# A second spectrum buffer, another priority and a last matmul group by column halves, in a one-core FFT convolution with gated MLP

## The chip, the cores and the metric

The kernel runs on one core of one Trainium2 chip. The metric is the device time of one launch in microseconds (us). A core has a matrix engine (TensorE, PE in the profile; PEld is its weight load), a vector engine (VectorE, DVE), a scalar engine (ScalarE, ACT), GpSimd (POOL), and SyncE (SP), which here only issues transfers.

## The reference

Two sequential blocks with pre-normalisation on a sequence of 2048 rows and 640 channels, in bf16:

```python
x = A_u                                           # (1, 2048, 640)
h  = x + conv(layernorm(x))                       # state space kernel K, applied by FFT of length 4096
h2 = h + ((sigmoid(n @ w_gate) * (n @ w_up)) @ w_down)   # n = layernorm(h), inner width 1728
```

The kernel works on four blocks of 512 rows. The convolution of a block is a product of spectra (inputs Z, kernel spectra S) followed by an inverse transform on TensorE; for block 0 that happens in four channel chunks of 160 (numbered 0 to 3), interleaved with the tail of the making of K. The MLP of a block follows when its normalisation is ready.

## The kernel before

A scheduler orders the instructions of each engine by priority and by its own idea of when they become ready. The order in the engine queues is then fixed at build time.

The product spectrum V of one chunk of block 0 has one buffer (tag `t3`, one slot), so chunk c+1 may write V only when the inverse transform of chunk c has read it:

```python
def prod(c, fs):
    if not fs[0]:
        T["y", c] = prp.tile([P, 2, 2, 2, W], BF16, name="V", tag="t3", bufs=1)
    ...
    V(g(t1[:, f]), z, k, ALU.mult)                               # L536
    V(g(t2[:, f]), z, k[:, :, ::-1], ALU.mult)                   # L537
    V(y[:, f, :, 0], t1[:, f, :, 0], t1[:, f, :, 1], ALU.subtract)   # L538
    V(y[:, f, :, 1], t2[:, f, :, 0], t2[:, f, :, 1], ALU.add)        # L539
```

The last chunk is done at a raised priority, and statistics of the chunks that are already finished are put in around it:

```python
    for r in range(4):
        for q in range(NC - 2):                     # chunks 0 and 1
            nc.vector.bn_stats(st2[:, r, q, :], h[:, r, W * q:W * q + W])   # L712
    tc.cur_priority += int(AT["EARLY"])
    piece(1, 0, 0, ...)                             # first piece of block 1's products: L693 to L704
    tc.cur_priority -= int(AT["EARLY"])
    tc.cur_priority -= int(AT["TAIL"])              # 64
    spec(c, 0, 0)
    spec(c, 0, 1)
    prod(c, (0,))                                   # first half of V of chunk 3
    prod(c, (1,))                                   # second half
    tc.cur_priority += int(AT["TAIL"])
    ... # bn_stats of chunk 2 (L723); then the inverse, with bn_stats of chunk 3 straight from PSUM (L727)
```

The last stage of the MLP is the down projection. Its output for a row group of 128 rows has two column halves of 320, in the two banks of one PSUM tile:

```python
po = [[t[:, c] for c in range(2)] for t in (pso_p.tile([P, 2, 512], F32, ...) for _ in range(2))]
def chunks(k, start, stop):
    lr = lp + k
    for ft in range(FT):                            # 13
        for c in range(2):
            nc.tensor.matmul(po[k][c][:, 0:320], lhsT=hm[:, ft, ...], rhs=Wd[:, ft, 320 * c:320 * c + 320], ...)
...
    for k in range(2):
        for c in range(2):
            nc.vector.tensor_tensor(h2[:, c], ..., h2[:, c], ALU.add)
        if b == NB - 1:
            nc.sync.dma_start(oh[b, :, lr:lr + 1, :], hs[b][:, lr:lr + 1, :])
```

## Time and profile before

| | before |
|---|---|
| time, median of the first 3 runs (range) | 356.66 us (356.56 to 356.86) |
| span of the profiled execution | 355.0 us |
| busy: PE, DVE, ACT | 320.4, 283.3, 245.9 us |
| last L341 to the L727 statistics | 125.87 to 144.34: 18.47 us |
| L727 to the end of the last matmul | 144.34 to 351.42: 207.08 us |
| end of the last matmul to the end of the span | 351.42 to 355.0: 3.58 us |

The mark "last L341" is the last instruction of the K tables on VectorE; up to 120 us, shortly ahead of it, nothing that the change edits has run (the first is chunk 1's V, at 120.76).

Lines that come up often: L536 and L537 make the factors of V, the product of spectra, and L538 and L539 V itself; L565 are the matmuls of the inverse transform (ps_y) and L568 is ScalarE's copy of their result; L518 are the matmuls that make the kernel's spectra and L522 ScalarE's copies of these (S, xk); L580 is a small product for the block's edge, which the inverse also needs; L712, L723 and L727 are statistics; L693 to L704 belong to block 1; L909 are the gate (ml_pg) and up (ml_pu) matmuls of the MLP.

The lines that the change moves are these, from the timeline of VectorE of the kernel before. The columns are start, length, engine, line, operation, output and inputs, forms and count; brackets at the end tell how long the engine was idle before and what ended it.

```profile
141.13 0.32 DVE L539 TENSOR_TENSOR V<-t 128x320 bf16<-128x320 bf16 x1
141.47 0.23 DVE L580 TENSOR_TENSOR edge<-edge,uhead 1x160 bf16<-1x160 bf16 x1
141.73 0.49 DVE L702 TENSOR_TENSOR early<-VR 128x640 bf16<-128x640 bf16 x1
142.14 0.32 DVE L723 BATCH_NORM_STATS2 ln_st<-h 128x6 f32<-128x160 bf16 x1
142.38 0.88 DVE L704 TENSOR_TENSOR VR<-early 128x640 bf16<-128x640 bf16 x2
143.17 0.77 DVE L723 BATCH_NORM_STATS2 ln_st<-h 128x6 f32<-128x160 bf16 x3
144.34 1.03 DVE L727 BATCH_NORM_STATS2 ln_st<-ps_y 128x6 f32<-128x160 f32 x4 [0.40 <-PE ps_y L565]
```

V of chunk 3 is whole at about 141.45; the edge product, L702 and the two L704 stand behind it and run while TensorE makes the inverse. L727 starts when TensorE has finished, after 0.40 us of idleness.

### The profile page before, as it was taken

The page shows a single profiled execution, that of the slowest core. Times are in us where ns is not written, and L with a number is a line of the kernel's source. Part 1 is how long each engine was busy: PE and PEld are TensorE (multiplying, and loading weights), DVE is VectorE, ACT ScalarE, POOL GpSimd, SP SyncE. Part 2 cuts the span into 40 slices and gives each one's busy share as a digit, 9 for nine tenths or more (in the row PEclk, how much of TensorE's full clock was granted, in tenths as well). Part 3 has the DMA queues.
Part 4 walks back from the last instruction along what each step waited for, and adds up shares of the span by engine and source line. Part 5 has one row for each costly group of instructions (what it writes and reads, how often), then busy time and mean ns, then how long its engine had stood idle before and what let it go on. Part 6 is the DMA issues. An engine that isn't in the chain of part 4 may idle for free.

```text
span 355.0 us, 6617 instructions
## 1 busy us (share of the span) xinstructions
PE 320.4 (90%) x2584; PEld 204.0 (57%) x2584; DVE 283.3 (80%) x570; ACT 245.9 (69%) x455; POOL 11.4 (3%) x20
## 2 busy tenths in 40 slices
PE   2587989997799999899999899998899999999995
PEld 1464667765487778755456554555554456544463
DVE  3899999999898799879999899999899951211222
ACT  6999999998999764673767845547844678455500
POOL 1020002200000000100000100000100001000000
PEclk9998999999999999999999999999999999999999
DMA  6990000454205339989500053000012000400011
GB/s 172 323 404 4 15 2 2 113 179 157 76 3 160 137 88 352 289 273 280 227 4 0 5 179 113 3 0 0 3 74 76 0 1 11 133 7 1 0 37 38
DMA packets 32391, 35.00 MB, mean 99 GB/s; under 512 B 19676, under 2 KB 27741, under 8 KB 32104
## 3 DMA queue, kind: packets, MB, share of 16 engines
q1 hardware_dynamic: 32360, 34.59, 30.7%
q8 instruction: 20, 0.33, 0.4%
q14 instruction: 11, 0.09, 0.1%
HBM read 24.70 MB, written 9.21 MB: 96 GB/s over the span
## 4 chain that ended last, share of the span: by engine, by line
DVE 28%; PE 18%; issue 14%; ACT 2%; POOL 1%; POOLq 0%; DVEq 0%; ACTq 0%
DVE u L694 5%; PE ml_po L942 5%; DVE u L693 5%; PE ml_pg L909 5%; PE ml_pu L909 4%; DVE u L696 3%; DVE u L697 3%; DVE ml_hm L920 2%; DVE VR L704 2%; PE ps_y L565 1%; DVE Z L673 1%; DVE y L701 1%; DVE y L702 1%; DVE h L805 1%; ACT ln L859 1%
## 5 line engine op out<-in xcount | busy, mean ns | idle before, releaser
L909 PE MATMUL ml_pg<-lnT,Wg 128*128 128x512 bf16 x260 | 64.6, 379 | 0.2 <-ACT ml_sg L917 0.2
L909 PE MATMUL ml_pu<-lnT,Wu 128*128 128x512 bf16 x260 | 64.4, 379 | 0.0
L942 PE MATMUL ml_po<-Wd,ml_hm 128*128 128x320 bf16 x416 | 59.5, 299 | 1.7 <-ACT Wd L963 1.7
L942 PEld LDWEIGHTS <-ml_hm 128*128 128x128 bf16 x416 | 40.1, 98 | 19.6 <-issue 3.7
L917 ACT ACTIVATE ml_sg<-ml_pg 128x512 bf16<-128x512 f32 x52 | 30.9, 597 | 25.5 <-PE ml_pg L909 11.9
L920 DVE TENSOR_TENSOR ml_hm<-ml_ub,ml_sg 128x512 bf16<-128x512 bf16 x52 | 22.0, 423 | 28.0 <-ACT ml_ub L919 28.0
L909 PEld LDWEIGHTS <-Wu 128*128 128x128 bf16 x260 | 25.4, 98 | 30.7 <-issue 0.3
L919 ACT CAST ml_ub<-ml_pu 128x512 bf16<-128x512 f32 x52 | 30.4, 584 | 17.0 <-PE ml_pu L909 16.9
L909 PEld LDWEIGHTS <-Wg 128*128 128x128 bf16 x260 | 25.4, 98 | 28.8 <-issue 0.4
L457 PE MATMUL ps_z<-u,c_G 128*128 128x320 bf16 x192 | 30.3, 307 | 4.5 <-ACT zs L458 2.7
L518 PE MATMUL ps_xk<-kv,c_KM 128*128 128x160 bf16 x320 | 27.0, 232 | 1.8 <-ACT S L522 0.8
L693 DVE TENSOR_TENSOR u<-Z,S 128x1280 bf16<-128x1280 bf16 x34 | 27.8, 820 | 0.0
L694 DVE TENSOR_TENSOR u<-Z,S 128x1280 bf16<-128x1280 bf16 x34 | 27.8, 820 | 0.0
L457 PEld LDWEIGHTS <-c_G 128*128 128x128 bf16 x192 | 18.9, 99 | 13.7 <-issue 6.0
L518 PEld LDWEIGHTS <-c_KM 128*128 128x128 bf16 x320 | 23.5, 98 | 4.5 <-issue 3.5
L247 PE MATMUL ps_t<-fr,c_dg 128*128 128x160 f16 (+1 forms) x180 | 19.7, 240 | 4.9 <-DMA c_dg<-s4c_dg 4.1
L247 PEld LDWEIGHTS <-c_dg 128*128 128x128 f16 x180 | 14.9, 100 | 11.4 <-DMA c_dg<-s4c_dg 4.7
L697 DVE TENSOR_TENSOR u<-u,u 128x1280 bf16<-128x1280 bf16 x23 | 18.9, 821 | 0.1
L696 DVE TENSOR_TENSOR u<-u,u 128x1280 bf16<-128x1280 bf16 x23 | 18.9, 821 | 0.0
L476 PE MATMUL pk<-tabB,tabA 128*128 128x84 bf16 x320 | 16.1, 200 | 1.8 <-ACT kts L477 1.4
L477 ACT CAST kts<-pk 128x420 bf16<-128x420 f32 x32 | 15.9, 558 | 1.8 <-PE pk L476 1.8
L476 PEld LDWEIGHTS <-tabA 128*128 128x128 bf16 x320 | 14.3, 97 | 4.8 <-issue 3.3
(158 smaller groups left out, 546.1 us busy)
## 6 DMA issues: line engine op xcount, KB each, us to landing
dz<-zs SPq DMA_DIRECT2D x12, 320.0 KB, 2.4
c_KM<-s4c_KM SPq DMA_DIRECT2D x1, 2560.0 KB, 12.6
dxk<-xk SPq DMA_DIRECT2D x16, 160.0 KB, 3.8
h<-in_A_u_dram SPq DMA_DIRECT2D x4, 640.0 KB, 4.4
eo<-dz SPq DMA_DIRECT2D x4, 640.0 KB, 4.3
S<-dxk SPq DMA_DIRECT2D x4, 640.0 KB, 5.3
Wg<-in_B_w_gate_dram SPq DMA_DIRECT2D x4, 520.0 KB, 9.4
Wu<-in_B_w_up_dram SPq DMA_DIRECT2D x4, 520.0 KB, 8.5
```

The costliest lines, as they stand in the source:

```text
L247: MM(ps[:, a, q * w:q * w + w], lhsT=dg[:, dk, :], rhs=fr[:, src, i, o + oo:o + oo + w], start=False, stop=(q == m - 1 and i == 1))
L457: MM(ps[:, ri, 0:UH], lhsT=G[:, ft, 0 if b in EO else hf, ri, r, :], rhs=us[b][:, r, o:o + UH], start=(r == rr[0]), stop=(r == rr[-1]))
L476: MM(pk[:, i, :], lhsT=A[:, ri, g].rearrange("p e c -> p (e c)"), rhs=B[:, ri, :, 4 * g:4 * g + 4], start=(ri == 0), stop=(ri == 1))
L518: mm = MM(ps[:, hf, ri * W:ri * W + W], lhsT=KM[:, ft, hf, ri, KI[d] + q, :], rhs=kv[:, j, :], start=(q == 0), stop=(q == len(KD[d]) - 1)).ins
L693: V(t1, z, k[:, :, :, hs_], ALU.mult)
L694: V(t2, z, k[:, :, ::-1, hs_], ALU.mult)
L696: V(s1, s1, t1, ALU.add)
L697: V(s2, s2, t2, ALU.add)
L909: nc.tensor.matmul(ps[:], lhsT=W[:, dc, f0:f0 + 128], rhs=lnT[:, dc].rearrange("p a b -> p (a b)"), start=(dc == 0), stop=(dc == 4))
L917: nc.scalar.activation(sg[:], pg[:], AF.Sigmoid)
L919: nc.scalar.copy(ub[:], pu[:])
L942: nc.tensor.matmul(po[k][c][:, 0:320], lhsT=hm[:, ft, 128 * lr:128 * lr + 128], rhs=Wd[:, ft, 320 * c:320 * c + 320], start=(start and ft ...
```

## The change

Its intent: the V of chunks 1 and 3 go into another pool slot (tag `y`, two slots), so that a chunk needn't wait for the inverse of the one before; the raised priority of the last chunk, with this, is dropped; and the last row group computes its first column half whole, then its second, so that the first can be added and sent while the second is computed.

```diff
-      ... "TAIL": 64.2, ...
+      ... "TAIL": 0, ...
@@ prod
-            T["y", c] = prp.tile([P, 2, 2, 2, W], BF16, name="V", tag="t3", bufs=1)
+            T["y", c] = prp.tile([P, 2, 2, 2, W], BF16, name="V", **(dict(tag="y") if c % 2 else dict(tag="t3", bufs=1)))
@@ down projection
+            end = b == NB - 1 and lp
             def chunks(k, start, stop):
                 lr = lp + k
-                for ft in range(FT):
-                    for c in range(2):
-                        nc.tensor.matmul(po[k][c][:, 0:320], ...
+                for ft, c in [(ft, c) for c in range(2) for ft in range(FT)] if end and k else [(ft, c) for ft in range(FT) for c in range(2)]:
+                    nc.tensor.matmul(po[k][c][:, 0:320], ...
@@
+                    if end and k:
+                        nc.sync.dma_start(oh[b, :, lr, 320 * c:320 * c + 320], hv[:, 320 * c:320 * c + 320])
-                if b == NB - 1:
+                if b == NB - 1 and not (end and k):
                     nc.sync.dma_start(oh[b, :, lr:lr + 1, :], hs[b][:, lr:lr + 1, :])
```

Cut: a function `last_up` that holds the same instructions as before under a new name, and a mode `PW == 2` that the settings do not use. They shift the line numbers: the down projection L942 is L951 in the changed kernel, its adds L964 are L973, its gate and up matmuls L909 are L910.

## The prediction

> **What bounds the kernel now.** I read the page first (busy shares, 40 slices), then the chain that ended last in order of time, then the timeline of VectorE and TensorE in the two stretches that the diff touches: about 126 to 153 us, where the first block's last channel chunks are finished, and 336 to 355 us, the last down projection. The page says that no engine is the bound all the way:
>
> ```profile
> PE 320.4 (90%) x2584; PEld 204.0 (57%) x2584; DVE 283.3 (80%) x570; ACT 245.9 (69%) x455; POOL 11.4 (3%) x20
> ...
> PE   2587989997799999899999899998899999999995
> ...
> DVE  3899999999898799879999899999899951211222
> ```
>
> Each slice is 8.9 us. DVE stands at seven tenths or more from the second slice to the 32nd (to 284 us), mostly at nine; after that PE alone is full. The chain confirms it: from 133 us it hops along VectorE, with short pieces on PE, to 250 us; from about 302 us it is PE, and it ends so:
>
> ```profile
> 347.39 0.38 PE ml_po L953 x4
> 347.77 3.65 PE ml_po L942 x26
> 351.42 0.02 issue
> 351.44 0.49 DVE h L964
> 351.94 0.40 DVEq L1027
> ```
>
> In that view the columns are start, length and what. After the last down matmul the two 320-column halves of the last row group are both added, one after the other. The timeline has them as one row of 0.89 us:
>
> ```profile
> 351.44 0.89 DVE L964 TENSOR_TENSOR h<-ml_po,h 128x320 bf16<-128x320 f32 x2 [2.75 <-PE ml_po L942]
> ```
>
> Before it VectorE has been idle for 2.75 us, although with another order of the matmuls the first half could have been ready. The output transfer follows, and the span ends at 355.0.
>
> The first stretch is where the spectrum buffer matters. V (the product spectrum of a chunk of 160 channels) has one buffer. Chunk 2's factors are multiplied from 126.61 to 128.08, but V itself is written only once chunk 1's inverse has read its V to the end (chain):
>
> ```profile
> 130.94 2.06 PE ps_y L565 x28
> 133.00 0.02 issue
> 133.03 0.49 DVE V L538
> 133.52 0.40 DVE V L539
> ```
>
> So there is a true wait of the V write for PE, some 5 us in data terms. What was VectorE doing in those 5 us? Timeline again:
>
> ```profile
> 128.08 1.00 DVE L712 BATCH_NORM_STATS2 ln_st<-h 128x6 f32<-128x160 bf16 x4
> 129.18 1.56 DVE L673 TENSOR_TENSOR Z<-eo 128x1280 bf16<-128x1280 bf16 x2
> 130.66 0.82 DVE L693 TENSOR_TENSOR VR<-Z,S 128x1280 bf16<-128x1280 bf16 x1
> 131.40 0.82 DVE L694 TENSOR_TENSOR VR<-Z,S 128x1280 bf16<-128x1280 bf16 x1
> 132.13 0.82 DVE L693 TENSOR_TENSOR early<-Z,S 128x1280 bf16<-128x1280 bf16 x1
> ```
>
> It was full with other needed work. Busy time by stretch, from the windows view (DVE alone): 6.25 of 6.40 us from 126.6 to 133.0, 5.78 of 5.80 to 138.8, 5.10 of 5.50 to 144.3. The wait is hidden almost wholly, and that decides what removing it is worth.
>
> **What the Trainium skill says.** PSUM — Partial Sum Buffer, "Engine vs sequencer instructions": VectorE's queue is strict FIFO and matmuls start and complete in program order. The trace agrees as far as it can (V at 133.03 stands behind "early" at 132.13, in the built order), so I work from the order in which the two built programs list their instructions. Perfetto Trace Analysis, "Optimization Strategy": a repeated bubble on the engine that should be saturated can mean that buffers are too few. Here there is no such bubble on VectorE, which speaks against a large gain from a second buffer. DMA: Bandwidth & Descriptors, "Anatomy of one DMA": about 2.0 us fixed per transfer plus bytes over 436 GB/s. The trace agrees on the fixed part: the last block's output transfers (four of 164 KB) and the three of the earlier blocks land 1.8 to 2.9 us after issue, median 2.0.
>
> **The change part by part.** Instruction counts on PE, DVE and ACT are the same in both built programs; one output transfer is added. Only places in the queues change, and past the first block's end they are the same but for one gate matmul.
>
> *Second V buffer, chunk 1.* Chunk 1's V moves to the "y" slots, so its write (120.76 us) now waits for the transfer out of the slot's earlier tile, the third of the last four dz stores. That one is issued at 117.27; the landing of these four is 2.4 to 3.1 us, so it is free by about 120.4. Cost 0, at worst some tenths.
>
> *Second V buffer, chunk 2, and lost priority.* In the new order both V writes follow the factors at once (end 128.97 instead of 133.92), and four statistics instructions become one at first. VectorE then does Z, 693, one statistic, 694, 693 and reaches 133.14, just where it was before. But the next instruction is the statistics of chunk 1's output, which needs the ACT copy that starts at 133.02 and takes 0.69. So VectorE idles some 0.65 us and goes on at about 133.8: just when it does in the old order (133.84). The early V is paid back as idle time: 0 gained here.
>
> From 133.84 to the end of chunk 3's V the old order takes until 141.45. In the new order the same queue has more in front of that V: two more statistics (0.24 each), the edge product (0.24), L702 (0.40) and two L704 (0.40 each). These are start-to-start distances on the timeline and in the chain. Sum 0.48 + 0.24 + 0.40 + 0.80 = 1.92 us, so V ends at about 143.37. This is the lost priority: that work used to stand behind V.
>
> What V releases is chunk 3's inverse: edge matmul, then 32 matmuls in 2.32 us (141.98 to 144.30 on the chain), all after V was whole and the edge done. Now the edge comes early and the first half of V is ready at about 142.1, so 16 of the 32 (1.16 us) run beside the second half of V. After 143.4 there are 16 left: end about 144.6 instead of 144.30. The pushed-forward work no longer stands between V and the last statistics (four L723, about 1.0 us, end at about 144.35, beside the matmuls). Net **+0.3 us** at the statistics of L727, from 144.34 to about 144.65.
>
> PE itself: chunk 2's inverse now follows chunk 1's at once (133.25 + 32 x 0.07 = 135.5, was 137.0), then the last K diagonal (about 1.0), ACT's copy (0.5), and 24 spectrum matmuls (24 x 0.07 = 1.7) to about 138.9, with the last needed S copied at about 139.7. Old: 139.68. No gain, but VectorE asks for it only after 139.9, so no loss.
>
> Everything after L727 (variance, power on POOL, normalisation, transposes, first MLP block) hangs on it, and the old chain has no large slack afterwards, so +0.3 reaches the end.
>
> *Last down group by column halves.* The last 26 matmuls stay 26, with a weight load each as before; 13 per half in 1.83 us (3.65/2). The first half's add (0.49) and its 82 KB transfer run beside the second half's matmuls. After the last matmul one add is left rather than two: from the 0.89 us row to 0.49, **-0.40**. The last transfer is half as large: by the skill's rate an estimate of 164/436 - 82/436 = 0.19 us less, though rows of 640 rather than 1280 bytes may eat part; I take **-0.1**. The first half's issue (0.33 us on SP) is long over.
>
> Sum: +0.3 - 0.4 - 0.1 = -0.2 us; 356.66 - 0.2, about 356.4 us.
>
> **The rivals.** (a) The second buffer really pays: V was PE-blocked, and moving chunk 2's inverse forward by 1.5 us pulls the whole tail of the block forward. For it: the chain does pass through that wait at 133.03, and PE gets its work earlier. Against it: VectorE is 97 to 99% busy there, does the same work before L727 in both orders, and gains an idle of 0.65. It would give at most the present idle before L727 (0.40) and the 0.1 before Z, so 355.7 with the tail's gain. (b) The lost priority costs more: chunk 3's V late by 1.9 us with no overlap of the half-inverse (if the first 16 matmuls also wait for all of V, 144.3 + 1.9 - 0.2, or +1.5). For it: PE runs in order and one more wait in front is enough. Against it: the first inverse matmul waits for a count on VectorE at which only the first half need be there, as the source reads only that half. Time then 357.7. (c) The end gains nothing, because the last transfer's fixed 2 us and the closing barrier set it anyway. Against it: these follow the last add in series, so they move with it. Then 356.9. (d) Chunk 1's V waits for a dz store that lands late: VectorE is saturated there, so up to 0.5 us would go straight into the time.
>
> **Range and chances.** The two sure things are small and opposed: a gain of 0.4 to 0.6 at the end, a head change between -0.5 and +1.0. Added: -1.1 to +0.6, that is 355.6 to 357.2, the range I give. Two per cent is 7.1 us; nothing that the change touches is that large (the whole wait for V is 5 us and is covered), so faster or slower by that much gets 1% each.
>
> **What would show it.** V of chunk 2 starts near 128.1; a VectorE idle of about 0.6 us near 133.2, ended by ACT's copy of h; V of chunk 3 ends about 1.9 us later than 141.45, with L702 and L704 ahead of it; the L727 statistics start at 144.4 to 144.9. In the last 4 us: an add about 1.8 us before the last matmul ends, a single 0.49 us add after it. It is wrong if L727 starts before 144.0 (rival a) or after 145.3 (rival b), if the V of chunk 1 no longer starts at 120.8 (rival d), or if the distance from last matmul to the end of the span does not shrink.

## The result, and the profile after

| | before | after |
|---|---|---|
| time, median (range, runs) | 356.62 us (356.56 to 356.86, 4) | 356.67 us (356.25 to 357.8, 4) |
| span of the profiled execution | 355.0 | 355.0 |
| last L341 starts at | 125.87 | 125.38 |
| last L341 to L727 | 18.47 | 18.84 |
| L727 to the end of the last matmul | 207.08 | 207.23 |
| last matmul to the end of the span | 3.58 | 3.55 |

The ratio is 1.0005, with a 95% interval of 0.9981 to 1.0029. Ratios here are the mean time of one kernel's runs over that of the other's of the same rounds, so not quite the ratio of the medians that are quoted. The time lies in the predicted range, but the table says that it is not there for the predicted reasons: the first two stretches are longer by 0.37 and 0.15, and the last, from which 0.5 was to be gained, is not shorter. The two spans are equal only because the profiled execution of the changed kernel reached the first mark 0.49 us earlier.

The page of the changed kernel is that of before to a digit or two:

```profile
PE 321.2 (90%) x2584; PEld 204.2 (58%) x2584; DVE 283.4 (80%) x570; ACT 246.0 (69%) x455; POOL 11.4 (3%) x20
...
DVE  3899999999898899879999899999899951211221
```

The timeline of VectorE in the first stretch, changed kernel. Take the first mark, 125.38, from each start to compare with before (125.87 there):

```profile
120.60 0.49 DVE L538 TENSOR_TENSOR V<-t 128x640 bf16<-128x640 bf16 x1 [0.25 <-ACT h L568]
...
127.59 0.48 DVE L538 TENSOR_TENSOR V<-t 128x640 bf16<-128x640 bf16 x1
...
131.87 0.81 DVE L693 TENSOR_TENSOR early<-Z,S 128x1280 bf16<-128x1280 bf16 x1
133.26 0.78 DVE L712 BATCH_NORM_STATS2 ln_st<-h 128x6 f32<-128x160 bf16 x3 [0.57 <-ACT h L568]
...
139.09 0.48 DVE L702 TENSOR_TENSOR early<-VR 128x640 bf16<-128x640 bf16 x1
139.49 0.49 DVE L536 TENSOR_TENSOR t<-Z,S 128x640 bf16<-128x640 bf16 x1
139.89 0.89 DVE L704 TENSOR_TENSOR VR<-early 128x640 bf16<-128x640 bf16 x2
...
142.61 0.32 DVE L539 TENSOR_TENSOR V<-t 128x320 bf16<-128x320 bf16 x1
142.84 1.00 DVE L723 BATCH_NORM_STATS2 ln_st<-h 128x6 f32<-128x160 bf16 x4
144.22 1.02 DVE L727 BATCH_NORM_STATS2 ln_st<-ps_y 128x6 f32<-128x160 f32 x4 [0.37 <-PE ps_y L565]
```

The first line is chunk 1's V, told of below. V of chunk 2 is written at once, at 127.59. Some instructions later VectorE is idle for 0.57 us, until ScalarE has copied chunk 1's output: what the second buffer won is lost again. L702 and L704 now stand ahead of the V of chunk 3, which is whole at 142.93 (142.61 and 0.32), 17.55 us after the mark (before: 15.58). L727 still waits for TensorE, 0.37 us.

TensorE is as full as VectorE here. The chain of work that ended last runs through TensorE from 126.25 to 144.19, broken only by one copy of ScalarE (0.50 us) and some hundredths of issue. The first half of chunk 3's inverse ends at 142.98, when the second half of V (142.93) has only just come. So an earlier V alone would have moved L727 by a few hundredths at most; this is an estimate from these two times, and no run tried it.

At the end, the chain of work that ended last, and below it the adds and the last two transfers from the timeline, changed kernel:

```profile
347.80 3.65 PE ml_po L951 x26
351.45 0.02 issue
351.47 0.49 DVE h L973
351.97 0.40 DVEq L1038
```

```profile
351.47 0.89 DVE L973 TENSOR_TENSOR h<-ml_po,h 128x320 bf16<-128x320 f32 x2 [2.75 <-PE ml_po L951]
351.99 0.81 SPq L975 DMA_DIRECT2D out_dram<-h  x2
```

Both adds still come after all 26 matmuls, in one row of 0.89 us, and VectorE is idle before them for the same 2.75 us as before. The two half transfers are issued directly after one another. So the new order of the matmuls had no effect on the adds.

The reason can be read in the built program, without a chip. In the list of VectorE's instructions the first of these two adds waits for TensorE's count 2564, which is the count that the very last matmul brings it to, and the second waits for nothing. The wait is the same number in both kernels. The two halves are the two banks of one PSUM tile, so the explanation to be tested is that the dependence is kept for the tile.

The 0.15 us of the middle stretch sit in its first 13 us. In both timelines the gate matmuls of block 0's MLP start while ScalarE still empties the last spectra (xk). First before, then after:

```profile
152.39 2.68 ACT L522 CAST xk<-ps_xk 128x640 bf16<-128x640 f32 x4
...
152.61 1.46 PE L909 MATMUL ml_pg<-lnT,Wg 128*128 128x512 bf16 x6
...
155.51 2.33 PE L909 MATMUL ml_pu<-lnT,Wu 128*128 128x512 bf16 x10
```

```profile
152.47 1.67 PE L910 MATMUL ml_pg<-lnT,Wg 128*128 128x512 bf16 x7
...
154.46 0.69 ACT L522 CAST xk<-ps_xk 128x640 bf16<-128x640 f32 x1 [0.37 <-PE ps_xk L518]
...
155.56 2.33 PE L910 MATMUL ml_pu<-lnT,Wu 128*128 128x512 bf16 x10
```

Seven gate matmuls instead of six now stand ahead of the last four spectrum matmuls. ScalarE's fourth copy waits for those (0.37 us), and the up matmuls (ml_pu) start 11.34 us after L727 instead of 11.17: that is 0.17 us, all of the difference of the stretch.

### The profile page after: what moved, and what is told of

It is laid out like the page before. It is cut to its first block, busy times and chain, and to the rows that moved or that the text cites. A ratio compares the mean times of both kernels' runs of the same rounds, so it can differ in the third digit from the quotient of the medians. Undisturbed runs are those within 1.5% of the kernel's fastest.

```text
span 355.0 us, 6614 instructions
## 1 busy us (share of the span) xinstructions
PE 321.2 (90%) x2584; PEld 204.2 (58%) x2584; DVE 283.4 (80%) x570; ACT 246.0 (69%) x455; POOL 11.4 (3%) x20
## 4 chain that ended last, share of the span: by engine, by line
DVE 28%; PE 27%; ACT 25%; issue 16%; DMA 2%; POOL 1%; SPq 0%; POOLq 0%; DVEq 0%; ACTq 0%
DVE u L694 5%; PE ml_po L951 5%; DVE u L693 5%; PE ml_pg L910 4%; PE ml_pu L910 4%; DVE u L696 3%; DVE u L697 3%; PE ps_y L565 3%; ACT a_sn L274 2%; PE ps_xk L518 2%; ACT zs L458 2%; DVE ml_hm L931 2%; ACT tabEA L274 2%; DVE VR L704 2%; PE ps_kv L487 2%
## 5 line engine op out<-in xcount | busy, mean ns | idle before, releaser
L910 PE MATMUL ml_pg<-lnT,Wg 128*128 128x512 bf16 x260 | 64.6, 379 | 0.2 <-ACT ml_sg L928 0.2
L910 PE MATMUL ml_pu<-lnT,Wu 128*128 128x512 bf16 x260 | 64.4, 379 | 0.0
L951 PE MATMUL ml_po<-Wd,ml_hm 128*128 128x320 bf16 x416 | 59.5, 299 | 1.7 <-ACT Wd L972 1.7
L951 PEld LDWEIGHTS <-ml_hm 128*128 128x128 bf16 x416 | 40.1, 98 | 19.6 <-issue 3.7
L910 PEld LDWEIGHTS <-Wu 128*128 128x128 bf16 x260 | 25.3, 98 | 30.7 <-DMA h<-in_A_u_dram 0.3
L910 PEld LDWEIGHTS <-Wg 128*128 128x128 bf16 x260 | 25.3, 98 | 28.9 <-issue 0.4
L697 DVE TENSOR_TENSOR u<-u,u 128x1280 bf16<-128x1280 bf16 x23 | 18.8, 815 | 0.1
```

The costliest lines, as they stand in the source:

```text
L697: V(s2, s2, t2, ALU.add)
L910: nc.tensor.matmul(ps[:], lhsT=W[:, dc, f0:f0 + 128], rhs=lnT[:, dc].rearrange("p a b -> p (a b)"), start=(dc == 0), stop=(dc == 4))
L951: nc.tensor.matmul(po[k][c][:, 0:320], lhsT=hm[:, ft, 128 * lr:128 * lr + 128], rhs=Wd[:, ft, 320 * c:320 * c + 320], start=(start and ft ...
```

## The experiments

My theory after reading the result: the end gains nothing because of the dependence on the whole PSUM tile; the head loses 0.37 us, because VectorE is full, so that the new order only brings idleness and puts work ahead of V; the rest of a difference between whole times is noise of the first 125 us. The rivals: the end is set by the closing transfer; the second buffer or the lost priority alone is to blame; the start belongs to the build.

There were eleven runs, two of them of kernels already measured (e8, e12) and two that repeat an experiment (e13, e14), all with correct results, with five rounds each. For each, the stretches are those of its profile; spans are given to 0.1, so the last stretch is good to about 0.05 us. The packed traces keep the span to a nanosecond. With it the last stretch is 3.56 before, 3.59 in the changed kernel and again in e8, 3.07, 3.07 and 3.06 with halves in two tiles (e1, e5, e13) and 3.17 with one transfer (e6). "First mark" is the start of the last L341.

### The changed kernel with the halves in two PSUM tiles (e1_after_split)

```diff
-  po = [[t[:, c] for c in range(2)] for t in (pso_p.tile([P, 2, 512], F32, ...) for _ in range(2))]
+  po = [[t[:, c] for c in range(2)] for t in (pso_p.tile([P, 2, 512], F32, ...) for _ in range(1 if b == NB - 1 and lp else 2))]
+  if b == NB - 1 and lp:
+      po.append([psg_p.tile([P, 512], F32, name="ml_po", tag="ml_pg") for _ in range(2)])
```

> The changed kernel, with one thing added: the two column halves of the last row group accumulate in two separate PSUM tiles instead of the two banks of one tile. My theory: in the changed kernel both adds wait for the last matmul because the dependence is kept for the whole tile (the first add waits for the last matmul, the second for nothing). Then here the first add starts near the middle of the last 26 matmuls (about 1.8 us before the last ends), a single 0.49 us add follows the last matmul, and the stretch from the last matmul's end to the end of the span shrinks by 0.4 to 0.6 us; time about 0.4 us under the changed kernel. Rival 1 (the last transfer's fixed cost and the closing barrier set the end): the adds split, but the stretch stays within 0.1 us. Rival 2 (two accumulations cannot be read and written side by side for another reason): the first add still starts after the last matmul.

Measured: stretches 18.84, 207.25 and 3.07 us, first mark 125.84; 356.88 us median, ratio to before 1.0005 (0.9993 to 1.0017). In this kernel's timeline the adds are apart:

```profile
350.19 0.49 DVE L975 TENSOR_TENSOR h<-ml_po,h 128x320 bf16<-128x320 f32 x1 [0.99 <-PE ml_po L953]
351.95 0.49 DVE L975 TENSOR_TENSOR h<-ml_po,h 128x320 bf16<-128x320 f32 x1 [1.27 <-PE ml_po L953]
```

The first add starts 1.74 us before the last matmul ends at 351.93, and the end is 0.48 us shorter than in the changed kernel (3.55; 0.53 by the exact spans). Both rivals about the end fall: neither a fixed closing nor reading one bank beside writing another stands in the way. The whole time didn't show the gain; against before the stretches leave +0.37 + 0.17 - 0.51, or nothing. Kernels are compared only within the same rounds.

### Only the third part of the change (e2_tail_only)

The kernel before with the diff's parts for the down projection, one PSUM tile as in the change.

> The kernel before with only the third part of the change: last group by column halves in one PSUM tile, and its two half transfers. My theory: no gain, both adds in one 0.89 us row after the last matmul, two transfers issued one after the other; stretch from the last matmul to the end of the span as in the kernel before within 0.15 us, time ratio 1.000. The rival, that the halves gain and the first block loses it again, expects 0.4 to 0.6 us less than before here.

Measured: 18.47, 207.07 and 3.59 us; first mark 124.87; 356.12 us median, ratio 0.9987 (0.9975 to 0.9999). The stretches say, as expected, that this part does nothing: the adds are one row of 0.89 us, the transfers follow each other. The whole time missed my 1.000. The profile puts the difference ahead of the first mark, which came 1.00 us earlier than in before's profile, where both programs have the same queues. The rival's 0.4 to 0.6 us are in the time but not at the place that it names.

### Only the second buffer (e3_buffer_only)

```diff
-            T["y", c] = prp.tile([P, 2, 2, 2, W], BF16, name="V", tag="t3", bufs=1)
+            T["y", c] = prp.tile([P, 2, 2, 2, W], BF16, name="V", **(dict(tag="y") if c % 2 else dict(tag="t3", bufs=1)))
```

> The kernel before with only the second V buffer; priority kept. My theory: V of chunk 2 is written near 128 us and VectorE then idles about 0.55 us for ACT's copy of chunk 1's output, so nothing is gained; from the start of the last L341 to the start of the L727 statistics 18.3 to 18.8 us (before 18.47). If the second buffer really paid (rival), this is 17.9 or less.

Measured: 18.80, 207.59 and 3.54 us; first mark 125.97; 357.53 us median, ratio 1.0022 (1.0009 to 1.0035). So the second buffer alone makes the kernel slower, by 0.33 in the first stretch and 0.5 in the second (the first gate matmul starts 8.80 us after L727, in before 8.27). In its timeline of VectorE:

```profile
139.23 0.49 DVE L536 TENSOR_TENSOR t<-Z,S 128x640 bf16<-128x640 bf16 x1 [0.24 <-ACT S L522]
...
144.77 1.03 DVE L727 BATCH_NORM_STATS2 ln_st<-ps_y 128x6 f32<-128x160 f32 x4
```

There is the 0.57 us wait at the statistics again, then 0.24 more for chunk 3's spectrum. L727 has no bracket: it starts the moment VectorE has got through its queue. That doesn't make VectorE's queue the only bound, because TensorE's last inverse matmul ends at 144.73, just then. But the inverse waited for the edge product (0.29 us), which VectorE made 15.93 us after the mark instead of 15.60 (at 141.90, before at 141.47). So VectorE's lateness, 0.33 us, reaches L727 on either way.

### Only the priority (e4_prio_only)

```diff
-      ... "TAIL": 64.2, ...
+      ... "TAIL": 0, ...
```

> The kernel before with only the priority of the last chunk taken away; one V buffer. My theory: the work pushed before V (edge product, L702, two L704: 1.44 us) makes V end about 1.4 us later, but half of the inverse runs beside the second half of V and no idle at the statistics exists, so L727 starts 0.0 to 0.3 us EARLIER than before: 18.2 to 18.5 us from the start of the last L341 (before 18.47, changed kernel 18.84). Rival (the lost priority is what costs in the changed kernel): 18.8 us or more here.

Measured: 18.53, 207.46 and 3.52 us; first mark 126.19; 357.02 us median, ratio 1.0014 (0.9999 to 1.0029). The first stretch is 0.06 us longer, not shorter: outside my 18.2 to 18.5 by a little, but far from the rival's 18.8. V of chunk 3 is whole 17.24 us after the mark (before: 15.58), so it is late by 1.66 us, and nearly all of it is hidden, because half of the inverse runs beside the second half of V. From there to L727 it is 1.29 us here and in the changed kernel alike; in before it was 2.89, as the edge product and the whole inverse came after V. The middle stretch, of which I had expected nothing, is 0.38 us longer. Its order has eight gate matmuls ahead of the last four spectrum matmuls (the trace holds seven; one record seems to be missing, as the 1.73 us up to the first of the four fit eight), and the up matmuls start 11.57 us after L727. With before (six: 207.08 and 11.17) and the change (seven: 207.23 and 11.34) that makes three points in line, some 0.2 us for each gate matmul, which take 1.08 us for five.

### The changed kernel, more runs (e8_after_again)

> The changed kernel once more, unedited, with more runs. By the segments of its first trace it should be 0.5 us slower than before where the start is equal (0.37 up to the L727 statistics, 0.16 between these and the last matmul, nothing at the end): ratio 1.0015, with an interval of some 0.0015 either way. If instead the true difference is a gain, as I predicted (-0.2 us), the ratio is 0.9995 or less.

Measured: 18.84, 207.24 and 3.63 us; first mark 126.79; 357.34 us median (356.52 to 358.27, 6 runs), ratio 1.0017 (1.0002 to 1.0032). The stretches are those of the first profile within 0.01, but for the end (within 0.1, or 0.01 by the exact spans), while the first mark is 1.41 us later. The ratio fits the loss of 0.5 us and not a gain of 0.2. The median of these runs lies outside the predicted range, which ended at 357.2.

### The kernel before with only the end mended (e5_before_split, again as e13_split_again)

The down projection by halves as in the change, and the two PSUM tiles of the first experiment; buffer and priority as before. All three compute queues are those of before up to the order of the last 26 matmuls.

> The kernel before with only the last group by column halves, and the halves in two PSUM tiles. The queues are those of before up to the last group. My theory: the first block as before (18.47 us from the last L341 to L727), the stretch after the last matmul 3.07 us instead of 3.58; ratio 0.9986, about 0.5 us faster than before: the best of all. The rival, that the end is given back elsewhere or set by the closing, expects 1.000.

Measured: 18.47, 207.05 and 3.10 us; first mark 126.38; 356.66 us median, ratio 0.9999 (0.9987 to 1.0011). The end is as expected, the time isn't, and the mark is late. So it ran once more:

> The kernel before with the last group by column halves in two PSUM tiles, once more, unedited. Its first measurement gave 0.9999 though its trace ends 0.48 us shorter after the last matmul, with the last L341 at 126.38 us, late. If the late start was noise, the ratio now is about 0.9986 with the start near 125.9; if it belongs to the build, the start is again near 126.4 and the ratio 1.000. The end is 3.07 to 3.1 us in either case.

Measured: 18.47, 207.09 and 3.04 us; first mark 126.90; 356.10 us median (355.28 to 357.3, 6 runs), ratio 0.9974 (0.9960 to 0.9989). The time now is faster by more than the end explains, although the profiled execution had the latest mark of all. My expectation that a ratio of 0.9986 would go with a mark near 125.9 fell; the two numbers are of different executions, and the profiled one of six is no measure of the rest. The mean of the two ratios is 0.99865, which is what 0.5 us makes, but their intervals barely overlap (0.9987 to 1.0011, 0.9960 to 0.9989), so the gain rests on the stretches and not on the times.

### One transfer instead of two halves (e6_split_one_dma)

As e5, but without the lines that send halves.

> As the run before, but with one transfer of the whole row group after both adds, instead of two half transfers. It splits the gain at the end: the single add is worth 0.40, the smaller last transfer the rest. I expect 3.15 to 3.2 us from the last matmul to the end of the span (3.58 before, 3.07 with half transfers). If the half transfers were what counts, it stays at 3.5.

Measured: 18.46, 207.06 and 3.20 us; first mark 125.98; 356.59 us median, ratio 0.9993 (0.9981 to 1.0005). Of the 0.5 us at the end, the single add makes about 0.38 (3.58 to 3.20) and the smaller last transfer about 0.1 (to 3.10 and 3.04). A transfer of 160 KB lands 1.8 us after its issue, one of 80 KB after 1.6 us; the latter is the first half's, as the profile doesn't tell when the second landed. (KB are 1024 bytes here; they are the prediction's 164 and 82 KB.)

### Two tiles without the order (e11_tiles_only, again as e14_tiles_again)

The two PSUM tiles in the kernel before, whose matmuls alternate between the halves.

> The kernel before with only the two PSUM tiles; the matmuls of the two halves still alternate, one transfer. The first half is then complete one matmul (0.14 us) before the last. My theory: the first add starts 0.1 us earlier, the second follows it, so the stretch after the last matmul shrinks by about 0.1 us only, to 3.45: the tiles without the order gain next to nothing. If separate tiles alone were the cure, it comes to 3.1.

Measured: 18.45 us for the first stretch; the first add starts when the last matmul but one has ended, and from the matmul that releases it to the end of the span it is 3.56 us, so 3.42 from the last matmul (a matmul is 0.14 us: 3.65/26). First mark 125.08; 356.02 us median, ratio 0.9983 (0.9970 to 0.9996). The end is as expected, and tiles alone are not the cure; the time was better than 0.15 us can make it. Once more:

> The kernel before with only the two PSUM tiles, once more, unedited. Its first measurement gave 0.9983, more than the 0.15 us of its end can explain, with the last L341 early at 125.08 us. If that was noise, the ratio now is 0.9995 or so; if it belongs to the build, 0.998 again with the start near 125.1.

Measured: 18.47 us, and 3.60 us from the releasing matmul to the end (3.46 from the last); first mark 125.78; 356.56 us median, ratio 0.9991 (0.9976 to 1.0007). So the first ratio was probably luck of the start for the most part.

### A control: the kernel before against itself (e12_before_as_test)

> The kernel before, unedited, timed against itself: a control. By the traces so far the moment at which the last L341 starts (before which no queue differs in any kernel) moves between 124.9 and 126.8 us from profile to profile. If that is run-to-run noise in waits for transfers, this gives a ratio within 0.9985 to 1.0015 that may well miss 1.0000 by 0.0005 or more, and segments 18.47, 207.07 and 3.58 us. If the start is a fixed property of a build, its runs repeat those of before closely and the ratio is within 0.0003 of 1.

Measured: 18.47, 207.07 and 3.56 us; first mark 126.20; 356.68 us median against 356.97 for the same kernel, ratio 0.9997 (0.9984 to 1.0010). The unedited kernel repeats its stretches within 0.02 us and moves its mark by 0.33. Over all thirteen profiles the mark lies between 124.87 and 126.90, and it belongs to no build: the changed kernel had it at 125.38 and 126.79. What differs ahead of it in the traces are waits for transfers: ScalarE's wait for the stores of input spectra (dz) is 1.3 us in the profile of before, 0.2 in the first of the changed kernel and none in e2's, and the first weight load of the K phase waits 4.3 to 6.0 us for its constants. Why these vary was not tested.

## Why the prediction was right or wrong

The range held (356.67 in 355.6 to 357.2). That the range held was in part luck: the one gain that the prediction counted as sure did not come, and the median of the repeated runs, 357.34, lies outside. The predicted gain of 0.2 us was wrong: from the stretches, the change costs +0.37 + 0.16 + 0.0, or about 0.5 us, and the repeated measurement (1.0017) agrees. Step by step:

- *Chunk 1's V, cost 0.* Right, and by the wait that was named. In the first profile V started at 120.60 after 0.25 us of idleness. The view puts that down to ScalarE's copy L568, but V doesn't wait for this copy: in e1, with the same queue, V started at 120.73 and the copy ended at 120.92. The built program makes V wait for the stores, and the third of the four landed at 120.38 in the first profile, just before. So rival (d)'s wait was real; it cost nothing, because the next wait in the queue was shorter (0.27 instead of 0.61 us): from the L341 before it to the last L341 the two kernels take 5.84 and 5.85 us.
- *Chunk 2's V is paid back as idleness.* Right; 0.57 us measured for 0.65, ended by the copy that was named. The buffer alone (e3) showed that it is even a loss of 0.33 us. Rival (a) fell.
- *Chunk 3's V 1.92 us later, of which 0.3 remain.* Right: 1.97 and 0.37. That the second half of V overlaps with the first half of the inverse, against rival (b), is shown by e4, where 1.66 us of lateness cost 0.06. The parts add up: 0.33 for the buffer and 0.06 for the priority, 0.37 for both together.
- *"The same but for one gate matmul".* This was noted, and given no cost. It costs about 0.16 us by the reading above: one more gate matmul stands ahead of the last spectrum matmuls in TensorE's order and delays ScalarE's last copy, and in the chain of work the next TensorE step (L740) waits for this copy.
- *The end.* This is the step that failed, one of "the two sure things": "The first half's add (0.49) and its 82 KB transfer run beside the second half's matmuls." I checked that the order of the matmuls had changed, and not what the add waits for. The built program said so in advance: the second add of the pair had no wait of its own, so the first had to carry the wait for both. What the runs showed in its place: both adds started after the last matmul, and the last stretch was 3.55 us (3.58 before), 0.0 gained for 0.5. The worth of the step was right: with two PSUM tiles the add is 0.38 and the transfer 0.1, for 0.40 and 0.1.
- *Rival (c), "the end gains nothing",* came nearest in time (356.9), but for another cause than it gave: the last add and the transfer do move with the last matmul, once the wait is gone.
- *Slips in the working, on which nothing else rests.* The sum for TensorE, 135.5 + 1.0 + 0.5 + 1.7, is 138.7 and not 138.9; rival (b)'s 1.9 - 0.2 is 1.7 and not 1.5. The landings of 1.8 to 2.9 us are of whole transfers, bytes included, so they don't confirm a fixed part of 2.0 us; the page's fit is for transfers issued by GpSimd, and these are SyncE's.

Shown by experiments: the cause at the end, both ways (e1, e2, e11), and that buffer and priority don't pay (e3, e4). Read from traces only: the 0.16 us of the gate matmul, though three orders lie in line. That TensorE stands at the same bound as VectorE in the first stretch is read from a trace too. In e3's middle stretch 0.5 us is measured, and which of its reordered transposes causes it wasn't tried.

The version that is ahead of both is the kernel before with the halves in two tiles: 0.5 us by its stretches, twice; 0.9999 and 0.9974 by its times.

## What to carry to other kernels

When an order is changed so that a result is ready earlier, look up what its reader waits for: a reader whose partner has no wait of its own is waiting for both. A buffer takes away a wait, and this is worth only what the waiting engine was idle for; on a full engine the freed work displaces other work, and what then comes to the front may have to wait in turn. Where a change is worth less than the run-to-run spread, compare stretches between marks in the trace, as they repeat far better than whole times.

## What the Trainium skill lacked or had wrong

- DMA: Bandwidth & Descriptors, "Anatomy of one DMA", has about 2.0 us fixed plus bytes over 436 GB/s, fitted to transfers issued by GpSimd, and no such fit for SyncE's. Output transfers issued by SyncE landed after 1.8 us with 160 KB and 1.6 us with 80 KB. The slope agrees (0.2 us for 80 KB, 0.19 by the page); the fixed part here is about 1.4 us, an estimate (1.8 less 0.38 by the page's rate).
- Perfetto Trace Analysis, "Optimization Strategy", names repeated bubbles on the saturated engine as a possible sign of too few buffers. It has no word on the opposite case: a buffer's wait that other work covers wholly (VectorE 97% busy or more across it), where a second buffer cost 0.33 us up to L727.
- No page that I read says that a dependence may be kept for a whole PSUM tile, so that a reader of one bank waits for the writer of the other: 0.48 us at the end here, gone with two tiles and the matmuls in the order of the halves.
- No page that I read gives the spread of a launch's time. Identical queues reached the same instruction between 124.87 and 126.90 us, while the stretch of 18.47 us behind it repeated within 0.02 us in kernels that share its order.
